# Attention with relative bias, then routed experts: keys and queries transposed two pairs ahead, and a smaller bias table fetched on another queue

## The chip, the cores and the metric

The kernel runs on one core of a Trainium2 chip. The metric is the time of one execution on the device, in microseconds (us); the median of three runs before the change is 409.79.

## What is computed

The reference has two parts. The first is attention with a bias that depends on the distance of query and key alone, through a table of 32 buckets per head:

```python
scores = scale * np.matmul(q, k.transpose(0, 1, 3, 2))      # 8 batches, 8 heads, 576 x 576, head size 64
bias = bias_table[bucket]                                   # bucket = f(|i - j|); constant from 128 on
scores = scores + bias.transpose(2, 0, 1)[None]
attn = softmax(scores)
out = np.matmul(attn, v)
```

The second takes the 4608 rows of that output (512 wide), sends each to one of 8 experts by a hash of its token id, and computes `relu(x @ w1[e]) @ w2[e]` for it.

## The kernel before

**Pairs.** Two heads of one batch make a pair; the 32 pairs (8 batches of 4) are gone through in order. The 576 positions are kept as four tiles of 128 (two row blocks T, each split by parity c of the position, so that a DMA row holds an even and an odd position) and a remainder of 64, which is collected for all heads of a batch. A pair has five groups: group g < 4 is one key tile against 512 queries, group 4 holds the remainder queries and remainder keys.

**One group on TensorE (PE).** `products` (line 457) multiplies the transposed keys `kz` with the transposed queries `qt` into the PSUM tile `ps`, of which there are three. `scores` (line 438, through the helper `bias`) adds the bias: a product of a reversed identity with a slice of `btb`, a band that holds the bias of every offset for every head; the remainder uses `btr`. ScalarE then takes the exponential of `ps` into `att` (line 492). The products of `att` with the values `va` run about seven groups later, nine at a time, into `px` (line 523); VectorE divides them into `x_all` (lines 532, 533).

**Transposes.** `cast_qk` turns the float32 loads `qf`, `kf` into `qh`, `kh` on GpSimd (POOL); `transpose_qk(n)` has PE transpose them into one PSUM tile `pqk` (line 373), which VectorE copies into `kz` (line 379, two copies) and `qt` (line 385). `pqk` shares its PSUM buffer with every second `px`. For the remainders of a batch, `load_rest` (lines 202, 214), `cast_rest` (line 246, giving `qrh`, `krh`) and `transpose_rest` (line 392, giving `pr`) do the same; `transpose_rest(b + 1)` stands in the third pair of batch b, behind group 1, and its casts stand in the second pair.

**Order.** Each engine runs its own list in the order of the program text (a manual schedule). In the main loop `pair_start(n)` issues on SyncE (SP) the loads of pair n + 4, in the first pair of a batch the next batch's remainders, and in pairs 2 to 11 one zero fill of the buffer `t_xperm`; on POOL the casts of pair n + 2, and later the scatter of finished rows. `behind(n, g)` follows each group: at g = 3 it transposes pair n + 1. POOL casts the values of pair n + 1 at g = 2. The buffers `qf`, `kf`, `vf` exist four times, `kz` three times, `qh`, `kh` and `qt` twice.

**Start.** Before the loop, PE multiplies the bias table `tbl` with a one-hot table `ohsb` (three parities of 384 columns, one product each, line 588). ScalarE copies the result in two pieces into `ebsb`, writes it to the DRAM buffer `t_f` (line 599), and reads it back: `btb` of heads 0 and 1 (`load_band`, line 605), `btr` in eight reads of 32 rows (line 618), later `btb` of heads 2 to 7, all on ScalarE's DMA queue. Each read takes a window that slides by one element per partition. The loads of q, k and v go on SP.

**After the loop** the rows are gathered by expert (`xpn`), transposed (`xps`), and multiplied with `w1t` (line 788) and `w2t` (line 806); finished rows are scattered to the output.

Of the kernel before, what the change touches and what calls it, by code (L numbers as in the profile page):

```python
# [11 lines left out]
F32 = mybir.dt.float32  # L12
# [19 lines left out]
def kernel(  # L32
# [38 lines left out]
    bucket = _bucket_table(NB, MAXD, S)  # L71
    last = NB - 1
    GL = 3 * P
    OH_np = np.zeros((NB, 3, GL), dtype=np.float32)
    for dl in range(3):
        for y in range(GL):
            r = 2 * (y - GL // 2 + 1) + dl - 1
            OH_np[bucket[min(abs(r), S - 1)], dl, y] += 1.0
            OH_np[last, dl, y] -= 1.0
    OH_np = OH_np.reshape(NB, 3 * GL)  # L80
    I128_np = np.zeros((P, 3, P), dtype=np.float16)
    I128_np[:, 0] = np.eye(P)
    I128_np[:, 1] = np.eye(P)[::-1]
# [65 lines left out]
    with tc.tile_pool(name="at", bufs=1) as at, tc.tile_pool(  # L149
# [18 lines left out]
        rr = [at.tile([P, (NPAIR + 1) * RC], F16, name=f"rr{i}")  # L168
              for i in range(2)]
        btb = at.tile([P, H, 3, WB], F16, name="btb")  # L170
        btr = at.tile([P, NPAIR, 2, D + RU], F16, name="btr")
        te = at.tile([P, NGT], I32, name="te")
        cnt = at.tile([P, 2 * P], F16, name="cnt")
        msk = at.tile([P, NGT + E], F32, name="msk")
# [192 lines left out]
        def transpose_qk(n, eng=None):  # L367
            pqk = aux(1, [P, 2, KT * P], F16, "pqk")
            for i, src in enumerate((kh, qh)):
                for t in range(KT):  # L370
                    T, c = t // 2, t % 2
                    o = P * t if i == 0 else NT * P * c + P * T
                    nc.tensor.transpose(  # L373
                        out=pqk[:, i, o : o + P],
                        in_=src[n][:, t, :, :].rearrange("p h d -> p (h d)"),
                        identity=ident[:, :],
                    )
            for hh in range(2):
                nc.vector.tensor_copy(  # L379
                    out=kz[n % 3][D * hh : D * hh + D, hh, :],  # L380
                    in_=pqk[D * hh : D * hh + D, 0, :],
                )
            kts[n] = kz[n % 3]
            qt = at.tile([P, KT * P], F16, name="qt", bufs=2)
            nc.vector.tensor_copy(out=qt[:, :], in_=pqk[:, 1, :])  # L385
            qts[n] = qt

# [30 lines left out]
        def rest_rest(b):  # L418
            prr = aux(0, [P, NPAIR, RC], F32, "prr")
            for m in range(NPAIR):  # L420
                nc.tensor.matmul(
                    out=prr[:, m, :], lhsT=kzr[b % 2][:, m, :],
                    rhs=qtr[b % 2][:, m, :], start=(m == 0), stop=True,
                    skip_group_check=True,
                )
            bias(
                prr[:, :, :].rearrange("p m (o u) -> p m o u", o=2),
                btr[:, :, :, D : D + RU], 2,
            )
            nc.scalar.activation(  # L430
                out=rr[b % 2][:, : NPAIR * RC].rearrange(
                    "p (m x) -> p m x", m=NPAIR
                ),
                in_=prr[:, :, :], func=AF.Exp, bias=0.0, scale=scale,
            )
# [27 lines left out]
        def scores(n, g):  # L463
            b, m = pairs[n]
            ps, att, qt = pss.pop((n, g)), atts[n], qts[n]
            T, c = g // 2, g % 2
            for hh in range(2):
                head = 2 * m + hh
                if g < KT:
                    x0 = D * T  # L470
                    bias(
                        ps[:, hh, :].rearrange("p (o u) -> p o u", o=2)[
                            :, :, x0 : x0 + BW
                        ],
                        btb[:, head, 1 - c : 3 - c,
                            D * (1 - T) : D * (1 - T) + BW], 1,
                    )
                    continue
                nc.tensor.matmul(
                    out=ps[:, hh, 2 * P :], lhsT=kzr[b % 2][:, m, :],  # L480
                    rhs=qt[:, 2 * P * hh : 2 * P * hh + 2 * P],
                    start=False, stop=True, skip_group_check=True,
                )
                for t in range(KT - 2, KT):
                    bias(
                        ps[:, hh, RC * t : RC * t + RC].rearrange(
                            "p (o u) -> p o u", o=2
                        ),
                        btb[:, head, 1 - t % 2 : 3 - t % 2, BW : BW + RU], 1,
                    )  # L490
                bias(ps[:, hh, 512 - D :], btr[:, m, hh, :D], 2)
            nc.scalar.activation(  # L492
                out=att[:, g, :, :], in_=ps[:, :, :],
                func=AF.Exp, bias=0.0, scale=scale,
            )
# [74 lines left out]
        load(0, "k")  # L570
        tbl = at.tile([NB, H], F32, name="tbl")
        nc.scalar.dma_start(out=tbl[:, :], in_=bias_table)
        ohsb = at.tile([NB, 3 * GL], F32, name="ohsb")
        nc.scalar.dma_start(out=ohsb[:, :], in_=OH_d.ap())
        nc.scalar.dma_start(out=idents[:, :, :], in_=I128_d.ap())
        load(0, "q")
# [2 lines left out]
        def z_init(i):  # L579
            nc.gpsimd.memset(kz[i][D:P, 0, :], 0.0)  # L580
            nc.gpsimd.memset(kz[i][:D, 1, :], 0.0)

        z_init(0)
        cast_qk(0, nc.vector, nc.vector)
        bps = [slot("bps") for _ in range(2)]
        ebsb = at.tile([H, 3, GL], F16, name="ebsb")
        for i in range(3):
            nc.tensor.matmul(
                out=bps[i // 2][:H, i % 2, :GL], lhsT=tbl[:, :],
                rhs=ohsb[:, GL * i : GL * i + GL],  # L590
            )
        for i in range(2):
            w = 2 - i
            nc.scalar.activation(
                out=ebsb[:, 2 * i : 2 * i + w, :],
                in_=bps[i][:H, :w, :GL], func=AF.Copy, bias=0.0,
                scale=1.0 / scale,
            )
# [5 lines left out]
        def load_band(h0, h1):  # L604
            nc.scalar.dma_start(
                out=btb[:, h0:h1, :, :].rearrange("p h a w -> p (h a) w"),
                in_=bass.AP(
                    F_d.ap().tensor, h0 * 3 * GL,
                    [[1, P], [GL, 3 * (h1 - h0)], [1, WB]],
                ),  # L610
            )

        load_band(0, 2)
        for hh in range(2):
            for c in range(2):
                for o in range(2):
                    r0 = D * hh + RU * c
                    nc.scalar.dma_start(
                        out=btr[r0 : r0 + RU, :, o, :],
                        in_=bass.AP(  # L620
                            F_d.ap().tensor,
                            (3 * hh + o - c + 1) * GL + P - RU,
                            [[1, RU], [6 * GL, NPAIR], [1, D + RU]],
                        ),
                    )
        transpose_qk(0)
        load(0, "v")
        load(1, "qk")
        for i in range(2):
            nc.gpsimd.memset(kzr[i][:, :, :].bitcast(I32), 0)  # L630
            nc.gpsimd.memset(vt[i][:, :, :].bitcast(I32), 0)
# [8 lines left out]
        for i in range(3):  # L640
            nc.gpsimd.memset(va[i][:, :, D : D + 1], 1.0)
        cast_v(0)
        load_rest(0, "v")
        load(1, "v")
        cast_qk(1)
        z_init(1)
        cast_vrest(0)
        load_band(2, H)
        load(2)
        load(3)  # L650
        z_init(2)
        nc.sync.dma_start(out=msk[:, :], in_=MSK_d.ap())
# [31 lines left out]
        def pair_start(n):  # L684
            b, m = pairs[n]
            if n + 4 < NP:
                load(n + 4)
            if n == 4:
                route_load()
            if 2 <= n < 2 + FILLS:  # L690
                fill_table(n - 2)
            if b + 1 < B and m == 0:
                load_rest(b + 1)
            if n + 2 < NP:
                cast_qk(n + 2)
# [12 lines left out]
            if n == 22:  # L708
                load_w2(0)
            if n == 25:  # L710
                load_w1(1)
            if n == 28:
                load_w2(1)

        def behind(n, g):
# [12 lines left out]
                advance(av, 9)  # L728
            if g == 2 and n + 1 < NP:
                cast_v(n + 1)  # L730
            if g == 3 and n + 1 < NP:
                transpose_qk(n + 1)

        for n in range(NP):
            pair_start(n)
            for g in range(NIT):
                products(n, g)
                scores(n, g)
                behind(n, g)
        advance(av, 99)  # L740
        assert not waiting
        guard.__exit__(None, None, None)
# [215 lines left out]
```

## Time and profile before

| | |
|---|---|
| median of three runs | 409.79 us (408.8 to 410.69) |
| profiled execution | 408.63 us, of which the span of the trace is 406.7 |
| mean granted TensorE clock | 0.972 of full speed |
| busy: PE / ScalarE / POOL / VectorE | 86% / 52% / 41% / 33% of the span |
| DMA | 72.66 MB, 179 GB/s in the mean |
| start, up to ScalarE's first exponential | 0 to 24.0 us |
| attention pairs | to about 231 us |
| gap until the first expert product | to about 250 us |
| experts | to 406.7 us |

Busy times are sums over stages that have different limits; what a wait is worth is read from the stage in which it stands. Line numbers are those of the kernel before.

### The profile page before, as it was taken

How to read it: one execution, taken by the hardware profiler on the slowest of the kernel's cores; microseconds unless marked ns; L12 is line 12 of the kernel's file. 1: busy time of each engine (PE TensorE's matmuls, PEld its weight loads, DVE VectorE, ACT ScalarE, POOL GpSimd, SP SyncE). 2: the span in 40 equal slices, each digit the busy share in tenths (PEclk: the TensorE clock that was granted, in tenths of full speed). 3: DMA queues.
4: the chain of work that ended last, by engine and by line, in shares of the span. 5: the costliest groups of instructions: out<-in, count | busy, mean ns of one | idle time of the engine just before them, and what ended most of it. 6: DMA issues, size and time to landing. Idle time of an engine off the chain costs nothing.

```text
span 406.7 us, 9256 instructions
## 1 busy us (share of the span) xinstructions
PE 351.2 (86%) x3792; PEld 229.0 (56%) x3792; DVE 136.2 (33%) x339; ACT 211.4 (52%) x235; POOL 167.1 (41%) x248
## 2 busy tenths in 40 slices
PE   4278999899999999999999807999999999999990
PEld 1035666566666666666666605665657575656650
DVE  1211346544434444344443401323140413223220
ACT  2046877687787877878778601322415051423320
POOL 3713225242576666583846040152333515151331
PEclk9998999999999999999999966999999999999997
DMA  6795967969685755997984025399999999995211
GB/s 172 192 244 147 266 134 215 272 189 269 196 237 169 206 176 134 249 186 212 235 174 94 10 77 175 53 204 159 258 161 266 201 193 261 160 264 115 89 70 61
DMA packets 95107, 72.66 MB, mean 179 GB/s; under 512 B 16295, under 2 KB 86183, under 8 KB 95056
## 3 DMA queue, kind: packets, MB, share of 16 engines
q0 software_dynamic: 17664, 30.96, 36.1%
q1 hardware_dynamic: 72880, 38.98, 35.1%
q10 hardware_dynamic: 4512, 2.04, 2.0%
q8 instruction: 32, 0.52, 0.5%
q14 instruction: 19, 0.16, 0.1%
HBM read 69.27 MB, written 21.03 MB: 222 GB/s over the span
## 4 chain that ended last, share of the span: by engine, by line
PE 71%; DVE 10%; DMA 8%; ACT 4%; issue 2%; SPq 2%; POOL 1%; POOLq 0%; ACTq 0%; DVEq 0%
PE hps L788 17%; PE ops L806 17%; PE ps L457 13%; PE ps L438 9%; PE px L523 8%; DVE kz L379 6%; ACT att L492 3%; PE pqk L373 3%; DVE qt L385 3%; PE xps L767 2%; DMA btb<-t_f 2%; DMA qf<-in_q_dram 2%; DMA xpn<-t_xperm 1%; DMA btr<-t_f 1%; SPq L188 1%
## 5 line engine op out<-in xcount | busy, mean ns | idle before, releaser
L492 ACT ACTIVATE att<-ps 128x1024 f16<-128x1024 f32 x160 | 161.7, 1023 | 58.6 <-PE ps L438 41.8
L794 ACT ACTIVATE h<-hps 128x640 f16<-128x640 f32 x64 | 45.0, 704 | 112.9 <-PE hps L788 112.9
L457 PE MATMUL ps<-qt,kz 128*128 128x512 f16 x256 | 78.9, 391 | 15.4 <-DVE qt L385 13.9
L438 PE MATMUL ps<-btb,idents 128*128 128x384 f16 (+1 forms) x384 | 78.2, 288 | 8.8 <-DMA btb<-t_f 8.8
L806 PE MATMUL ops<-w2t,h 128*128 128x512 f16 x320 | 72.7, 379 | 0.0
L788 PE MATMUL hps<-xpt,w1t 128*128 128x320 f16 x512 | 72.1, 301 | 0.1
L523 PEld LDWEIGHTS <-att 128*128 128x128 f16 x1408 | 61.0, 98 | 18.6 <-ACT rr L430 3.5
L523 PE MATMUL px<-va,att 128*128 128x65 f16 x1280 | 64.6, 193 | 1.2 <-DVE rcp L532 0.4
L438 PEld LDWEIGHTS <-idents 128*128 128x128 f16 x456 | 39.7, 100 | 42.0 <-issue 12.4
L814 POOL DMA_INDIRECT out_dram<-ok,xpn x40 | 39.2, 980 | 57.4 <-DVE ok L813 51.3
L788 PEld LDWEIGHTS <-w1t 128*128 128x128 f16 x512 | 50.4, 99 | 21.2 <-issue 0.3
L379 DVE COPY kz<-pqk 64x512 f16<-64x512 f16 x64 | 27.0, 422 | 77.6 <-PE pqk L373 76.6
L806 PEld LDWEIGHTS <-h 128*128 128x128 f16 x320 | 30.8, 98 | 33.4
L548 POOL DMA_INDIRECT t_xperm<-x_all,ds x40 | 39.4, 985 | 21.9 <-DVE rcp L532 11.3
L813 DVE COPY ok<-ops 128x512 f32<-128x512 f32 x40 | 27.7, 692 | 47.0 <-PE ops L806 47.0
L457 PEld LDWEIGHTS <-kz 128*128 128x128 f16 x512 | 28.2, 99 | 22.2 <-DVE qt L385 18.7
L771 DVE COPY xpt<-xps 128x640 f16<-128x640 f16 x32 | 15.0, 488 | 74.2 <-PE xps L767 59.7
L226 POOL CAST qh<-qf 128x512 f16<-128x512 f32 x31 | 19.0, 613 | 42.9 <-PE pqk L373 25.5
L533 DVE TENSOR_TENSOR x_all<-px,rcp 128x384 f16<-128x384 f32 x64 | 31.4, 491 | 2.2
L234 POOL CAST va<-vf 128x512 f16<-128x512 f32 x32 | 20.0, 624 | 28.5 <-PE px L523 15.7
L132 POOL DMA_DIRECT2D w1t<-in_moe_w_dram x8 | 6.5, 810 | 52.0 <-PE xps L767 51.9
L532 DVE RECIPROCAL rcp<-px 128x6 f32<-128x6 f32 x64 | 11.7, 183 | 42.4 <-PE px L523 42.4
(72 smaller groups left out, 243.0 us busy)
## 6 DMA issues: line engine op xcount, KB each, us to landing
kf<-in_k_dram SPq DMA_DIRECT2D x64, 128.0 KB
qf<-in_q_dram SPq DMA_DIRECT2D x64, 128.0 KB
vf<-in_v_dram SPq DMA_DIRECT2D x64, 128.0 KB
w1t<-in_moe_w_dram POOLq DMA_DIRECT2D x8, 1024.0 KB, 9.6
w2t<-in_moe_w_dram POOLq DMA_DIRECT2D x8, 1024.0 KB, 10.4
t_xperm<-zx SPq DMA_DIRECT2D x10, 514.0 KB
xpn<-t_xperm SPq DMA_DIRECT2D x8, 642.5 KB
btb<-t_f ACTq DMA_DIRECT2D x1, 1152.0 KB
```

The costliest lines, as they stand in the source:

```text
L379: nc.vector.tensor_copy(out=kz[n % 3][D * hh : D * hh + D, hh, :], in_=pqk[D * hh : D * hh + D, 0, :],)
L438: nc.tensor.matmul(out=out, lhsT=idents[:, which, :], rhs=rhs, start=False, stop=True, skip_group_check=True,)
L457: nc.tensor.matmul(out=ps[:, hh, o : o + rhs.shape[1]], lhsT=lhsT, rhs=rhs, start=(g < KT or t == 0), stop=True, skip_group_check=True,)
L492: nc.scalar.activation(out=att[:, g, :, :], in_=ps[:, :, :], func=AF.Exp, bias=0.0, scale=scale,)
L523: nc.tensor.matmul(out=po, lhsT=lhsT, rhs=rhs, start=(i == 0), stop=(i == len(todo) - 1), skip_group_check=True,)
L533: nc.vector.tensor_tensor(out=x_all[:, b, its[0] : its[0] + ni, :DM].rearrange("p t (m h d) -> p t m h d", h=2, m=NPAIR)[:, :, m, :, :], i ...
L548: sc_in = nc.gpsimd.indirect_dma_start(out=xperm_d.ap()[:, :], out_offset=bass.IndirectOffsetOnAxis(ap=ds2[:, B * t + b : B * t + b + 1], ...
L788: nc.tensor.matmul(out=hps[:, nr, :NR], lhsT=w1h[:, kt, ts(ft, P)], rhs=xt[e][:, kt, ts(nr, NR)], start=(kt == 0), stop=(kt == NPT - 1),)
L794: nc.scalar.activation(out=h1[:, ft, :].rearrange("p (r n) -> p r n", r=NRC), in_=hps[:, :, :NR], func=AF.Relu, bias=0.0, scale=1.0,)
L806: nc.tensor.matmul(out=ops[:, :], lhsT=h1[:, ft, ts(kc, P)], rhs=w2h[:, ft, :], start=(ft == 0), stop=(ft == NFT - 1),)
L813: nc.vector.tensor_copy(out=ok[:, :], in_=ops[:, :])
L814: so = nc.gpsimd.indirect_dma_start(out=out[:, :], out_offset=bass.IndirectOffsetOnAxis(ap=xn[e][:, kc, DM:XW].bitcast(I32), axis=0), in_= ...
```

## The change

The loads, casts and transposes keep their places in the loop but work for a later pair: the casts of pair n + 3 and the transposes of pair n + 2 stand where those of n + 2 and n + 1 stood, with a third `qt`. Pair 1 is transposed after the first group of pair 0, and pair 2 is cast before the loop. The one-hot table holds only the 129 columns per parity in which the bias differs from its far value; the rest of `ebsb` is zeroed by a memset on POOL. One product and one copy take the place of three and two. `btr` becomes a tile with a row of 480 elements per head pair, read by four transfers on SP; both parities are slices (`bro`) of that row. The band of heads 0 and 1 stays on ScalarE's queue, heads 2 and 3 and heads 4 to 7 are read on SP. In SP's order the loads of v of pair 0 and q, k of pair 1 stand before the `btr` reads, the remainders and pair 1's v after the second band.

```diff
-    OH_np = np.zeros((NB, 3, GL), dtype=np.float32)          # GL = 384
+    GN = MAXD + 1                                            # 129
+    OH_np = np.zeros((NB, 3, GN), dtype=np.float32)
...
-        btr = at.tile([P, NPAIR, 2, D + RU], F16, name="btr")
+        btr = at.tile([P, NPAIR, GL + D + RU], F16, name="btr")
+        bro = [btr[:, :, GL * o : GL * o + D + RU] for o in range(2)]
...
-            qt = at.tile([P, KT * P], F16, name="qt", bufs=2)
+            qt = at.tile([P, KT * P], F16, name="qt", bufs=3)
...                                                            # rest_rest
-            bias(prr[:, :, :].rearrange("p m (o u) -> p m o u", o=2), btr[:, :, :, D : D + RU], 2)
+            for o in range(2):
+                bias(prr[:, :, RU * o : RU * o + RU], bro[o][:, :, D : D + RU], 2)
...
+        ebsb = at.tile([H, 3, GL], F16, name="ebsb")
+        nc.gpsimd.memset(ebsb[:, :, :], 0.0)
...
-        for i in range(3):
-            nc.tensor.matmul(out=bps[i // 2][:H, i % 2, :GL], lhsT=tbl[:, :],
-                             rhs=ohsb[:, GL * i : GL * i + GL])
-        for i in range(2):
-            w = 2 - i
-            nc.scalar.activation(out=ebsb[:, 2 * i : 2 * i + w, :], in_=bps[i][:H, :w, :GL], ...)
+        bps = slot("bps")
+        nc.tensor.matmul(out=bps[:H, 0, : 3 * GN], lhsT=tbl[:, :], rhs=ohsb[:, :])
+        nc.scalar.activation(out=ebsb[:, :, P - 1 : P - 1 + GN],
+                             in_=bps[:H, 0, : 3 * GN].rearrange("h (a b) -> h a b", a=3), ...)
...
-        load_band(0, 2)
+        load_band(0, 2, nc.scalar)
+        load(0, "v")
+        load(1, "qk")
         for hh in range(2):
             for c in range(2):
-                for o in range(2):
-                    r0 = D * hh + RU * c
-                    nc.scalar.dma_start(out=btr[r0 : r0 + RU, :, o, :], in_=bass.AP(
-                        F_d.ap().tensor, (3 * hh + o - c + 1) * GL + P - RU,
-                        [[1, RU], [6 * GL, NPAIR], [1, D + RU]]))
+                r0 = D * hh + RU * c
+                nc.sync.dma_start(out=btr[r0 : r0 + RU, :, :], in_=bass.AP(
+                    F_d.ap().tensor, (3 * hh + 1 - c) * GL + P - RU,
+                    [[1, RU], [6 * GL, NPAIR], [1, GL + D + RU]]))
         transpose_qk(0)
-        load(0, "v")
-        load(1, "qk")
...
         cast_v(0)
+        cast_qk(1)
+        z_init(1)
+        load_band(2, 4, nc.sync)
         load_rest(0, "v")
         load(1, "v")
-        cast_qk(1)
-        z_init(1)
         cast_vrest(0)
-        load_band(2, H)
         load(2)
+        load_band(4, H, nc.sync)
+        cast_qk(2)
         load(3)
...                                                            # pair_start, behind, main loop
-            if n + 2 < NP:
-                cast_qk(n + 2)
+            if n + 3 < NP:
+                cast_qk(n + 3)
...
-            if g == 3 and n + 1 < NP:
-                transpose_qk(n + 1)
+            if g == 3 and n + 2 < NP:
+                transpose_qk(n + 2)
...
                 behind(n, g)
+                if (n, g) == (0, 0):
+                    transpose_qk(1)
```

## Rows read from the trace of the kernel before

**Rows 1.** The chain that ended last, shares of the span by engine.
```profile
PE 71%; DVE 10%; DMA 8%; ACT 4%; issue 2%; SPq 2%; POOL 1%; POOLq 0%; ACTq 0%; DVEq 0%
```

**Rows 2.** Waits for `qt`: whole run, PE from 66.3, PE from 93 (us, times, longest).
```profile
PE ps L457 <- DVE qt L385: 13.9, 31, 1.0
...
PE ps L457 <- DVE qt L385: 11.4, 25, 1.0
...
PE ps L457 <- DVE qt L385: 9.0, 21, 0.4
```

**Rows 3.** Busy times in stretches of four pairs (PE, PEld, DVE, ACT, POOL, clock, DMA, GB/s).
```profile
40.64:66.28 25.64, 23.84 (x351) 16.69 (x349) 11.96 (x34) 20.51 (x22) 7.44 (x14) 1.00 0.76 192
...
93.00:118.58 25.58, 23.77 (x351) 16.69 (x350) 10.92 (x31) 20.52 (x22) 12.62 (x20) 1.00 0.86 225
```

**Rows 4.** Timeline between two pairs (start, us, engine, line, idle before).
```profile
103.91 0.42 DVE L385 COPY qt<-pqk 128x512 f16<-128x512 f16 x1
...
104.39 0.61 PE L457 MATMUL ps<-qt,kz 128*128 128x512 f16 x2 [0.43 <-DVE qt L385]
...
105.16 0.43 PE L523 MATMUL px<-va,att 128*128 128x65 f16 x9
```

**Rows 5.** Timeline of ScalarE and its DMA queue (ACTq) at the start.
```profile
8.49 0.48 ACT L594 ACTIVATE ebsb<-bps 8x384 f16<-8x384 f32 x1 [0.48 <-PE bps L588]
10.92 0.50 ACTq L599 DMA_DIRECT2D t_f<-ebsb  x1
13.24 0.45 ACTq L605 DMA_DIRECT2D btb<-t_f  x1
13.73 9.29 ACTq L618 DMA_DIRECT2D btr<-t_f  x8
...
24.02 3.79 ACT L492 ACTIVATE att<-ps 128x1024 f16<-128x1024 f32 x4 [15.05 <-DMA btr<-t_f]
```

**Rows 6.** Timeline of PE at the start.
```profile
4.46 3.99 PE L588 MATMUL bps<-ohsb,tbl 32*8 32x384 f32 x6 [4.46 <-DMA ohsb<-t_bias_oh]
...
19.74 0.80 PE L438 MATMUL ps<-btb,idents 128*128 128x384 f16 x2 [6.68 <-DMA btb<-t_f]
...
25.09 1.01 PE L457 MATMUL ps<-qt,kz 128*128 128x512 f16 x2 [1.57 <-ACT att L492]
...
31.80 0.48 PE L438 MATMUL ps<-btb,idents 128*128 128x384 f16 x2 [2.11 <-DMA btb<-t_f]
```

**Rows 7.** Timeline of SyncE's DMA queue (SPq) at the start.
```profile
7.34 0.98 SPq L188 DMA_DIRECT2D kf<-in_k_dram  x2
...
15.83 3.21 SPq L188 DMA_DIRECT2D qf<-in_q_dram  x2
...
27.06 5.24 SPq L202 DMA_DIRECT2D qr<-in_q_dram  x2
```

**Rows 8.** SyncE's own waits: whole run, then 60 to 100, then 100 to 235.
```profile
SPq L202 <- DMA btb<-t_f: 4.1, 1, 4.1
...
SPq L188 <- POOL va L234: 0.6, 1, 0.6
...
SPq L188 <- POOL va L234: 13.9, 6, 3.1
```

**Rows 9.** Timeline of GpSimd: the casts of the remainder keys.
```profile
37.27 0.40 POOL L246 CAST krh<-kr 128x256 f16<-128x256 f32 x1 [1.79 <-DMA kr<-in_k_dram]
...
64.59 0.40 POOL L246 CAST krh<-kr 128x256 f16<-128x256 f32 x1 [1.55 <-DMA kr<-in_k_dram]
...
88.75 0.40 POOL L246 CAST krh<-kr 128x256 f16<-128x256 f32 x1 [1.38 <-DMA kr<-in_k_dram]
```

**Rows 10.** Timeline of PE: the transposes of the remainder keys.
```profile
40.64 0.27 PE L392 MATMUL pr<-idents,krh 128*128 128x128 f16 x2
...
66.28 0.28 PE L392 MATMUL pr<-idents,krh 128*128 128x128 f16 x2
...
93.00 0.27 PE L392 MATMUL pr<-idents,krh 128*128 128x128 f16 x2
```

More of the change, by code (lines that the diff above doesn't have):

```diff
@@ L73 @@
     GL = 3 * P
-    OH_np = np.zeros((NB, 3, GL), dtype=np.float32)
+    GN = MAXD + 1
+    OH_np = np.zeros((NB, 3, GN), dtype=np.float32)
     for dl in range(3):
-        for y in range(GL):
-            r = 2 * (y - GL // 2 + 1) + dl - 1
+        for y in range(GN):
+            r = 2 * y - MAXD + dl - 1
             OH_np[bucket[min(abs(r), S - 1)], dl, y] += 1.0
             OH_np[last, dl, y] -= 1.0
-    OH_np = OH_np.reshape(NB, 3 * GL)
+    OH_np = OH_np.reshape(NB, 3 * GN)
     I128_np = np.zeros((P, 3, P), dtype=np.float16)
@@ L170 @@
         btb = at.tile([P, H, 3, WB], F16, name="btb")
-        btr = at.tile([P, NPAIR, 2, D + RU], F16, name="btr")
+        btr = at.tile([P, NPAIR, GL + D + RU], F16, name="btr")
+        bro = [
+            btr[:, :, GL * o : GL * o + D + RU] for o in range(2)
+        ]
         te = at.tile([P, NGT], I32, name="te")
@@ L425, in rest_rest @@
                 )
[L426 to L429, printed above, removed]
+            for o in range(2):
+                bias(
+                    prr[:, :, RU * o : RU * o + RU],
+                    bro[o][:, :, D : D + RU], 2,
+                )
             nc.scalar.activation(
@@ L490, in scores @@
                     )
-                bias(ps[:, hh, 512 - D :], btr[:, m, hh, :D], 2)
+                bias(ps[:, hh, 512 - D :], bro[hh][:, m, :D], 2)
             nc.scalar.activation(
@@ L572 @@
         nc.scalar.dma_start(out=tbl[:, :], in_=bias_table)
-        ohsb = at.tile([NB, 3 * GL], F32, name="ohsb")
+        ohsb = at.tile([NB, 3 * GN], F32, name="ohsb")
+        ebsb = at.tile([H, 3, GL], F16, name="ebsb")
+        nc.gpsimd.memset(ebsb[:, :, :], 0.0)
         nc.scalar.dma_start(out=ohsb[:, :], in_=OH_d.ap())
@@ L584 @@
         cast_qk(0, nc.vector, nc.vector)
-        bps = [slot("bps") for _ in range(2)]
-        ebsb = at.tile([H, 3, GL], F16, name="ebsb")
-        for i in range(3):
[L588 to L591, printed above, removed]
-        for i in range(2):
-            w = 2 - i
[L594 to L598, printed above, removed]
+        bps = slot("bps")
+        nc.tensor.matmul(
+            out=bps[:H, 0, : 3 * GN], lhsT=tbl[:, :], rhs=ohsb[:, :],
+        )
+        nc.scalar.activation(
+            out=ebsb[:, :, P - 1 : P - 1 + GN],
+            in_=bps[:H, 0, : 3 * GN].rearrange("h (a b) -> h a b", a=3),
+            func=AF.Copy, bias=0.0, scale=1.0 / scale,
+        )
         nc.scalar.dma_start(
@@ L602, with load_band @@
         )
-        def load_band(h0, h1):
-            nc.scalar.dma_start(
+        def load_band(h0, h1, eng):
+            eng.dma_start(
                 out=btb[:, h0:h1, :, :].rearrange("p h a w -> p (h a) w"),
@@ L611, in load_band @@
             )
-        load_band(0, 2)
+        load_band(0, 2, nc.scalar)
+        load(0, "v")
+        load(1, "qk")
         for hh in range(2):
             for c in range(2):
-                for o in range(2):
-                    r0 = D * hh + RU * c
[L618 to L625, printed above, removed]
+                r0 = D * hh + RU * c
+                nc.sync.dma_start(
+                    out=btr[r0 : r0 + RU, :, :],
+                    in_=bass.AP(
+                        F_d.ap().tensor, (3 * hh + 1 - c) * GL + P - RU,
+                        [[1, RU], [6 * GL, NPAIR], [1, GL + D + RU]],
+                    ),
+                )
         transpose_qk(0)
-        load(0, "v")
-        load(1, "qk")
         for i in range(2):
```

## The prediction

> **What bounds the kernel now.** I read the chain of work that ended last first. TensorE (PE) carries 71% of the span, but 10% lies on VectorE, which a kernel bound by products alone would not show [rows 1]. The waits say where that comes from: the first product of a pair, line 457, waits for the copy `qt` 31 times, 13.9 us in total [rows 2]. Then the stretches by batch: from one batch's `pr` transposes to the next, four pairs take 25.6 us, of which PE is busy 23.8, and ScalarE 20.5 [rows 3]. The 1.8 us between are four waits of 0.45. One of them in the timeline: `qt` is copied 103.91 to 104.33, and the next pair's first product starts at 104.39 after 0.43 us of idling [rows 4]. So the middle of the kernel is PE work plus one exposed copy for each pair.
>
> The start is another matter, read from ScalarE's queue. It ends the second half of `ebsb` at 8.97, but issues the write of `t_f` at 10.92, spends 13.73 to 23.02 on issuing eight `btr` reads, then the large `btb` read, and does its first exponential at 24.02, after 15.05 us of idling that the view puts down to `btr` [rows 5]. PE waited 6.68 us to 19.74 for the first band, 1.57 to 25.09 for ScalarE and 2.11 to 31.80 for the second band [rows 6]. SyncE's queue (SP) has holes of its own: the two `qf` issues at 15.83 take 3.21 us, and the two `qr` issues at 27.06 take 5.24 us [rows 7], where two undisturbed ones take about 1.0; 4.1 us of the latter is a wait for `btb`, a transfer that `qr` has no data from [rows 8]. An issue can thus stand for an older, unrelated transfer.
>
> Last, what would be late if PE came earlier. PE needs the casts of the remainders, `krh`, at its `pr` transposes. For batches 1, 2 and 3 GpSimd starts that cast at 37.27, 64.59 and 88.75, after idling for the transfer [rows 9], and PE starts `pr` at 40.64, 66.28 and 93.00 [rows 10]. With the cast's 0.40 the spare time is 2.97, 1.29 and 3.85 us.
>
> **The change, part by part.** *Transposes and casts two pairs ahead.* No instruction is added: eight transposes and three copies per pair stay at the same place behind group 3, only for the pair after. The copy `qt` then has a whole pair to finish in, covered by about 5.9 us of PE work (23.8 / 4), so the 31 waits go to nothing. If they came back, each would cost 0.45. What is late next on PE is the first `px` that needs the same PSUM buffer: it stands at 105.16 with the wait, so at 104.73 without it, and the copy ends at 104.33 [rows 4]; 0.4 us is left. ScalarE's 20.5 us per batch fits into 23.8. On GpSimd the casts keep their place in each pair; what they need is loaded one pair less ahead. 25 of the waits, 11.4 us, come after the `pr` of batch 2 at 66.28; of these 9.0 come after that of batch 3 at 93.00 [rows 2].
>
> *One-hot product and the write of `t_f`.* Six partial products over 3 x 384 columns take 3.99 us [rows 6]; 387 columns are two of them, 1.33. Two copies become one, of 387 columns like the 0.48 us one of 384 [rows 5]. `ebsb` is thus ready near 4.46 + 1.33 + 0.48 = 6.3 instead of 8.97. The write may be held by an older transfer, as it was for 1.95 us: issue at 6.3 to 8.5. In the old run it let `btb` go at 13.24, 2.3 us after its issue [rows 5]; so the band's read goes out at about 8.6 to 10.8, some 3.5 us earlier. The added memset on GpSimd lies in its idle start.
>
> *`btr` in four reads on SP, the large band in two, both on SP.* ScalarE loses 9.3 us of issuing, so its first exponential follows the first band. PE's own lead, if nothing else were late, is by 66.28: 3.5 (band) + 1.6 (the wait for ScalarE) + 2.1 (second band) + 2.5 (the 31 - 25 copies before 66.28, 13.9 - 11.4) = 9.7 us [rows 2, 6].
>
> *What SP pays.* Four `btr` and two band reads come onto its queue: six issues at about 0.5, 3.0 us. The first stands before the write of `t_f` has landed; behind it wait the remainders of v, pair 1's v, pairs 2 and 3. The write lands 2.3 us after its issue, at 8.6 to 10.8; SP's last issue ahead of `btr` ends at 8.3 [rows 7], so it idles 0.3 to 2.5 us, say 1.1. The four reads move 480 columns per row for the 192 before, 491 KB for 197; the smaller one-hot table saves 98. Net 0.2 MB, about 0.9 to 1.0 us at the 192 to 225 GB/s of the batch stretches [rows 3], partly under SP's idle time: I take 0.3. What SP can win back is 4.1 us (the wait for `btb`, now split and earlier) and 2.2 us (the `qf` hole). Everything won would be 6.3; what I count as paid is 3.0 + 1.1 + 0.3 = 4.4. No row shows how the waits for older transfers fall in the new order; I take all 6.3 as won, because the long reads now stand further from `qr`, and so a lead of 6.3 - 4.4 = about 2 us. The bounds are -6 (nothing won; 3.0 + 2.5 + 0.9 paid) and +6 (all won, the new issues falling into SP's idle times).
>
> *Where PE meets SP.* From 60 to 100 us SP waited for GpSimd only 0.6 us [rows 8]: its loads come at their own pace and do not come faster because PE is ahead. Hence the remainders of batch 2 move by SP's lead only, and PE can be ahead at its `pr` by at most 1.29 + 2 = 3.3 us, though it would be 9.7 free. The other 6.4 us become new waits of PE: for `krh` of batch 1 first (2.97 + 2 = 5.0 at most), then batch 2. At batch 3 the limit is 3.85 + 2 = 5.85, and 3.3 + (11.4 - 9.0) = 5.7 passes just below. Past 100 us SP waits six times, 13.9 us, for the casts of v [rows 8], thus for compute, and the limit is gone. The eight batches' extra `prr` bias product (two of 128 columns for one of 256) costs at most 0.4 in all.
>
> Sum: 3.3 + 11.4 - 0.4 = 14.3 us. The profiled execution took 408.63 (span 406.7 and 1.9 around it), so 394.3; the median of the runs shown is 409.79, 1.16 above it, so 395.5.
>
> One rule speaks against the start's part of this. The Trainium skill, "DMA: Bandwidth & Descriptors", section "Issuing engines are not separate DMA queues", says that transfers started by different engines run on the same 16 DMA engines and interleave, so that another issuer saves only issue time, usually small beside the transfer. By that rule SP would have no lead, and the sum would be the second rival's below. The trace agrees only in part: the issue time was 9.29 us here [rows 5], not small.
>
> **The rivals.** *Transfers, not queues, set the pace.* The same bytes come when they came before, the lead is 0. Then PE gains 1.3 by batch 2, 3.7 by batch 3, and 9.0 - 0.4 after: 12.3 us, 397.5. For it: SP's free run and the DMA engines' 0.76 to 0.86 busy share in those stretches [rows 3]. Against it: SP's two holes, in which it issued nothing.
>
> *Supply hardly binds.* With SP's lead at its upper bound, 6, batch 2 allows 7.3, batch 3 then 7.3 + 2.4 = 9.7 (under 3.85 + 6): 9.7 + 9.0 - 0.4 = 18.3 us, 391.5. With 8.4 or more PE keeps all its 9.7: 9.7 + 11.4 - 0.4 = 20.7 us, 389. For it: the sum of the waits. Against it: spare times of 1.3 and 3.9 us.
>
> *SP comes out later.* With a lead of -6, batch 2 is at 1.29 - 6 = -4.7, batch 3 at -4.7 + 2.4 = -2.3, and 9.0 - 0.4 follow: 6.3 us, 403.5; with -3, 9.3 us, 400.5. For it: six more issues and the wait for `t_f` ahead of pairs 2 and 3.
>
> *The copy still holds PE,* by the shared PSUM buffer after it, when VectorE's routing steps or its divisions come in between. The 13.9 us stay, the start gives up to 1.3 + 2: near 407.5 to 409. Against it: 0.4 us of room.
>
> *Slower: SP behind `t_f`.* SP is one queue in order; if the reads of `btr` hold it until the old landing near 13.2 and every later issue waits for older transfers again, each microsecond of lateness past the spare time goes to PE one for one. By batch 2's row it decides from 1.29 + 11.4 - 0.4 = 12.3 us of lateness; at 14.5 the loss passes 0.5%, a time of 412. The rows bear out 6.
>
> **How the numbers follow.** My forecast 0.42 (393 to 397), no lead 0.20, supply hardly binds 0.14, SP later 0.14, the copy stays 0.05, slower 0.05. The likeliest gives 395.5. The first three and the nearer half of SP later hold 0.83, which gives 388.5 to 402 with the bounds of the lead. Faster by over 0.5% (2 us, about what a measurement of this kernel tells from no change): 0.42 + 0.20 + 0.14 + 0.14 + 0.01 = 0.91; within it 0.04; slower 0.05.
>
> **What would show it.** Right: no wait of line 457 for `qt`; four pairs in about 23.8 us late in the attention; first exponential near 17 instead of 24.02; new PE waits for `krh` at line 392 in pairs 2 and 6, together 5 to 7 us; the expert stage as long as before. Wrong: the `qt` wait replaced by one at line 523; no wait at line 392 (then the time is near 389 to 391); PE waits for `kh` or `btb` in pairs 0 to 3; SP's `qr` of batch 1 issued after 31.77.

## The result, and the profile after

The changed kernel took 395.24 us in the median of four runs (392.37 to 398.82), against 409.58 us for the kernel before beside it (408.80 to 410.69). Medians here are of all runs and ratios of the fast runs alone, without those over 1.5% above their kernel's fastest (398.82 here, three more in e10 and e11). The ratio is 0.9625, with a 95% interval of 0.9554 to 0.9695. Two later sets of six runs gave 398.49 us (ratio 0.9725, 0.9690 to 0.9759) and 395.90 us (0.9676, 0.9651 to 0.9701). The gain is therefore 10.5 to 14.3 us, and the changed kernel varies more from run to run than the one before. The profiled execution is the slowest of the first four: 398.82 us, a span of 396.7, which is 10.0 less than before. The two later profiles took 399.00 and 399.89, so all that is read from traces below explains a gain of about 10 us; what the executions of 392 to 396 us do differently, no trace shows. Line numbers moved on by 4 or 5 (188 is now 192, 392 is 396, 457 is 462, 523 is 528).

The chain of work that ended last, shares of the span by engine, answers to [rows 1]:

```profile
PE 52%; DMA 21%; SPq 13%; POOL 5%; issue 4%; DVE 2%; ACT 1%; POOLq 0%; DVEq 0%; ACTq 0%
```

VectorE, 10% before, is down to 2%. In its place the chain runs through transfers and SyncE's queue: 34% together, where it was 10%. Beside PE's own work, what set the end before was the exposed copy of each pair; now, for a third of the span, it is transfers and the queue that issues them, the supply of data.

TensorE's waits in the whole run (us, times, longest), against [rows 2]:

```profile
PE pr L396 <- POOL krh L250: 9.6, 3, 5.8
PE ps L443 <- DMA btb<-t_f: 4.0, 1, 4.0
...
PE px L528 <- DVE qt L389: 2.6, 1, 2.6
PE pqk L377 <- POOL kh L230: 2.5, 2, 1.4
```

The 31 waits of the first product for `qt` are gone without exception. New among the long ones are those for casts of loaded data, `krh` and `kh` on POOL, and one wait of `px`.

Stretches from one batch's `pr` to the next (columns as in [rows 3]):

```profile
91.41:114.57 23.16, 23.08 (x352) 16.71 (x351) 10.92 (x31) 20.43 (x22) 10.78 (x18) 1.00 0.81 230
114.57:137.72 23.15, 23.07 (x351) 16.71 (x350) 10.91 (x31) 20.53 (x22) 17.24 (x26) 1.00 0.69 199
137.72:160.88 23.16, 23.08 (x352) 16.72 (x350) 10.92 (x31) 20.54 (x22) 16.86 (x25) 1.00 0.88 219
```

Four pairs went from 25.6 to 23.16 us, so 0.60 to 0.62 for each pair, although the idle time that disappeared was only 0.45. Even PE's busy time fell, from 23.8 to 23.08, with no product left out. The timeline of PE between two pairs shows how:

```profile
101.24 0.35 PE L528 MATMUL px<-va,att 128*128 128x65 f16 x6
101.43 0.33 PE L528 MATMUL px<-vt,att 128*128 128x130 f16 x3
101.60 0.59 PE L462 MATMUL ps<-qt,kz 128*128 128x512 f16 x2
```

The same place in the kernel before; the row that follows it is the product at 104.39 in [rows 4]:

```profile
103.44 0.35 PE L523 MATMUL px<-va,att 128*128 128x65 f16 x6
103.63 0.33 PE L523 MATMUL px<-vt,att 128*128 128x130 f16 x3
```

From the start of the three `px` products to the start of the next product it was 104.39 - 103.63 = 0.76; now it is 101.60 - 101.43 = 0.17. The `px` group counts as busy for 0.33, but its successor starts after 0.17 when nothing holds it. The wait cost its idle 0.43 and also the 0.16 of overlap that was lost ahead of it.

The start: ScalarE with its DMA queue (against [rows 5]) in the timeline:

```profile
5.24 1.28 ACT L596 ACT_TABLE_LOAD   x1 [5.24 <-PE bps L593]
6.54 0.48 ACT L596 ACTIVATE ebsb<-bps 8x387 f16<-8x387 f32 x1
7.72 0.50 ACTq L601 DMA_DIRECT2D t_f<-ebsb  x1
10.87 0.43 ACTq L607 DMA_DIRECT2D btb<-t_f  x1
15.94 1.02 ACT L497 ACTIVATE att<-ps 128x1024 f16<-128x1024 f32 x1 [8.92 <-PE ps L443]
```

The first exponential comes at 15.94 where it came at 24.02. SyncE's queue (against [rows 7]):

```profile
10.87 1.76 SPq L621 DMA_DIRECT2D btr<-t_f  x4
...
16.90 1.54 SPq L192 DMA_DIRECT2D qf<-in_q_dram  x2
...
21.05 1.86 SPq L192 DMA_DIRECT2D qf<-in_q_dram  x2
22.95 1.91 SPq L192 DMA_DIRECT2D kf<-in_k_dram  x2
...
28.79 1.82 SPq L192 DMA_DIRECT2D kf<-in_k_dram  x2
...
31.73 1.15 SPq L206 DMA_DIRECT2D qr<-in_q_dram  x2
32.98 1.11 SPq L206 DMA_DIRECT2D kr<-in_k_dram  x2
```

The two long holes are gone, but four issues of two now take 1.5 to 1.9 us instead of 1.0, and `qr` of batch 1 still goes out only at 31.73 (before, its two issues stood in the queue from 27.06 to 32.30). So the casts of the remainder keys come when they came before (timeline of GpSimd, against [rows 9]):

```profile
37.78 0.40 POOL L250 CAST krh<-kr 128x256 f16<-128x256 f32 x1 [1.84 <-DMA kr<-in_k_dram]
64.76 0.40 POOL L250 CAST krh<-kr 128x256 f16<-128x256 f32 x1 [1.14 <-DMA kr<-in_k_dram]
88.22 0.40 POOL L250 CAST krh<-kr 128x256 f16<-128x256 f32 x1 [1.09 <-DMA kr<-in_k_dram]
```

And PE, which without the 5.75 us of waiting would reach batch 1's `pr` at 32.49, 8.15 us ahead of the kernel before, gives most of that back (timeline of PE, against [rows 10]):

```profile
38.24 0.40 PE L396 MATMUL pr<-idents,krh 128*128 128x128 f16 x2 [5.75 <-POOL krh L250]
65.22 0.28 PE L396 MATMUL pr<-idents,krh 128*128 128x128 f16 x2 [1.03 <-POOL krh L250]
91.41 0.28 PE L396 MATMUL pr<-idents,krh 128*128 128x128 f16 x2
...
187.01 0.29 PE L396 MATMUL pr<-idents,krh 128*128 128x128 f16 x2 [2.81 <-POOL krh L250]
```

PE is ahead of the kernel before by 2.40, 1.06 and 1.59 us at the `pr` of batches 1, 2 and 3, by 4.01, 6.43, 8.84 and 8.28 at those of batches 4 to 7, and by 10.8 at the first transpose of the expert stage (235.90 against 246.69).

### The profile page after: what moved, and what is told of

It is laid out like the page before. It is cut to its first block, busy times and chain, and to the rows that moved or that the text cites. A ratio compares the mean times of both kernels' runs of the same rounds, so it can differ in the third digit from the quotient of the medians.

```text
span 396.7 us, 9264 instructions
## 1 busy us (share of the span) xinstructions
PE 346.4 (87%) x3796; PEld 229.8 (58%) x3796; DVE 135.4 (34%) x339; ACT 210.6 (53%) x234; POOL 169.1 (43%) x249
## 4 chain that ended last, share of the span: by engine, by line
PE 52%; DMA 21%; SPq 13%; POOL 5%; issue 4%; DVE 2%; ACT 1%; POOLq 0%; DVEq 0%; ACTq 0%
PE hps L792 18%; PE ops L810 17%; SPq L192 6%; PE ps L462 5%; DMA vf<-in_v_dram 4%; PE px L528 4%; PE ps L443 3%; DMA kr<-in_k_dram 3%; DMA t_xperm<-zx 3%; SPq L206 3%; DMA kf<-in_k_dram 3%; PE xps L771 3%; DMA vr<-in_v_dram 2%; POOL t_xperm L553 2%; SPq L218 2%
## 5 line engine op out<-in xcount | busy, mean ns | idle before, releaser
L528 PE MATMUL px<-va,att 128*128 128x65 f16 x1280 | 65.5, 195 | 4.2 <-DVE qt L389 2.6
L792 PEld LDWEIGHTS <-w1t 128*128 128x128 f16 x512 | 50.8, 99 | 21.4
L462 PEld LDWEIGHTS <-kz 128*128 128x128 f16 x512 | 29.3, 99 | 0.8 <-issue 0.7
L771 PE MATMUL xps<-idents,xpn 128*128 128x128 f16 x160 | 13.9, 230 | 13.1 <-DMA xpn<-t_xperm 12.9
L238 POOL CAST va<-vf 128x512 f16<-128x512 f32 x32 | 19.9, 623 | 10.7 <-PE px L528 5.2
```

Of the source, the lines that this page charges most:

```text
L462: nc.tensor.matmul(out=ps[:, hh, o : o + rhs.shape[1]], lhsT=lhsT, rhs=rhs, start=(g < KT or t == 0), stop=True, skip_group_check=True,)
L528: nc.tensor.matmul(out=po, lhsT=lhsT, rhs=rhs, start=(i == 0), stop=(i == len(todo) - 1), skip_group_check=True,)
L792: nc.tensor.matmul(out=hps[:, nr, :NR], lhsT=w1h[:, kt, ts(ft, P)], rhs=xt[e][:, kt, ts(nr, NR)], start=(kt == 0), stop=(kt == NPT - 1),)
```

## The experiments

All were timed in five rounds beside the kernel before on their chip. The first four and the last four ran where the kernel before took 408.99 and 408.69 us; the middle four on a chip where it took 414.58, so they are compared by ratio; the changed kernel itself was not run on that chip. My theory: **supply**. PE's advance up to about 90 us is set by when SyncE's loads land; the start part of the change has nothing to give, and the gain is mainly the copies'. Its rivals: the start part brings part of the gain; or what is left is a matter of order, and other transfers ahead of the needed ones can be moved away.

**The changed kernel again (e0),** unedited.

> The changed kernel once more, for a second profile and a tighter ratio. Supply theory (SyncE's stream of loads sets when TensorE may pass the remainder transposes, about 38.2 and 65.2 us into the span whatever TensorE does): the wait for krh in pair 2 is again 5 to 6 us and the transposes of batch 2 start again within 1 us of 65.2; what differs between executions is the wait at batch 7 (2.8 us in the first profile) and the routing wait of 2.6 us at 73 us. Rival (clock theory: the half clock after the long wait is what moves the time between executions): the transposes of batch 2 start at a time that varies by 2 us or more. Time 392 to 397 either way.

398.49 us, ratio 0.9725 (0.9690 to 0.9759). PE's longest waits stand where they stood: 6.03 us before batch 1's `pr`, 2.66 at `px` in pair 6. The reference for the next three.

**The loop part alone (e1).** The kernel before with

```diff
-            if n + 2 < NP:
-                cast_qk(n + 2)
+            if n + 3 < NP:
+                cast_qk(n + 3)
...
-            if g == 3 and n + 1 < NP:
-                transpose_qk(n + 1)
+            if g == 3 and n + 2 < NP:
+                transpose_qk(n + 2)
...
+                if (n, g) == (0, 0):
+                    transpose_qk(1)
```

(with a third `qt`, and `cast_qk(2)` before the loop).

> The kernel before with the loop part alone: casts three pairs and transposes two pairs ahead, a third qt, pair 1 transposed behind the first group, pair 2 cast before the loop; one-hot table, btr and bands as before. Supply theory: the remainder keys land when they did before (37.1 and 64.5), TensorE passes batch 2's transposes at 65.1 to 65.5, and every later pair saves 0.45 to 0.6 us: 393 to 398, the same as the whole change within 3 us; the start part is worth nothing by itself. Rival (the start is worth the 7 to 8 us by which ScalarE's first exponential came earlier): 400 to 405, slower than the whole change by 5 us or more.

398.68 us, ratio 0.9721 (0.9686 to 0.9756): the whole change's 398.49 within 0.2. PE's waits:

```profile
PE ps L438 <- DMA btb<-t_f: 11.2, 2, 6.3
PE pr L392 <- POOL krh L246: 4.5, 2, 2.5
```

PE waits 11.2 us for the bands, 7.5 more than in e0, and yet the kernel ends as early: its waits for `krh`, for `kh` and of `px` for `qt` are 5.3 us together, where e0 has 14.2. What PE loses to the bands it doesn't lose to what comes late behind them.

**The start part alone (e2).** The changed kernel with the casts and transposes one pair later again (the edit above reversed).

> The whole change at the start (one-hot over 129 columns, one product and copy, btr in four reads and the later bands on SyncE, later loads), but casts two pairs and transposes one pair ahead in the loop as before, with pair 2's cast at pair_start(0) again. Supply theory: first exponential near 16 us, but batch 2's remainder transposes still at 65.2 to 66, and the 25 waits for qt after that are back: 0 to 1.5 us under the kernel before, 408 to 410. Rival (the start is worth 7 to 8 us): 401 to 403.

407.83 us, ratio 0.9969 (0.9956 to 0.9981): 1.2 us. PE's waits:

```profile
PE ps L462 <- DVE qt L389: 14.4, 31, 1.0
PE pr L396 <- POOL krh L250: 8.0, 1, 8.0
```

The first band's product is at 15.03 (it was at 19.74), and one wait of 8.0 us before 38.04 swallows it. e1 and e2 together decide for supply: the start is worth 1.2 us alone, and beside the loop part nothing that the runs can tell (0.2 us, where each ratio is uncertain by 1.4 us).

**The remainders a batch earlier (e3).** The changed kernel with

```diff
         load(3)
+        load_rest(1)
...
-            if b + 1 < B and m == 0:
-                load_rest(b + 1)
+            if b + 2 < B and m == 3:
+                load_rest(b + 2)
```

(and `cast_rest` ahead of `cast_qk`).

> The changed kernel with the remainders of a batch loaded earlier: batch 1's right after pair 3's loads, those of batch b + 2 in the last pair of batch b (so batch 2's ahead of the token loads of pair 4), and GpSimd casts the remainders ahead of the next keys and queries. No work is added. Supply theory: the waits for krh at batches 1, 2 and 7 (5.75 + 1.03 + 2.81 in the first profile) shrink to 0 at batches 2 and 7; at batch 1 part of it comes back as a wait of 1 to 4 us for kh, since the same bytes are in front; with a shorter idle the half clock after it goes too. 385 to 391. Rival (the remainders are not what binds; the loads of pairs 9 and later are as late): waits of the same length appear for kh in pairs 3 to 8, time within 2 us of the changed kernel.

396.05 us, ratio 0.9667 (0.9642 to 0.9692), 2.4 us under e0 where much more was expected. The waits for `krh` are down to 0.2 us (its casts at 31.51, 54.82 and 82.27), but others took their place. PE's waits:

```profile
PE pqk L377 <- POOL kh L230: 7.8, 4, 2.9
PE px L528 <- DVE qtr L413: 4.3, 1, 4.3
```

VectorE's wait behind the second of them:

```profile
DVE te L287 <- DMA te<-in_moe_token_ids_dram: 5.1, 1, 5.1
```

What was moved up pushed back what now stands behind it: the heads' own keys, and the token ids for the routing, on which VectorE stands with the copy `qtr` queued behind it.

**The routing later (e4).** The changed kernel with the steps of the routing in pairs 8 to 11 instead of 6 to 11, with the memsets of `keep` before the loop.

```diff
-            if 6 <= n < 12:
+            if 8 <= n < 12:
```

> The changed kernel with the routing steps on VectorE spread over pairs 8 to 11 instead of 6 to 11, and the two memsets of keep on GpSimd moved to the start. The order of the loads is as in the change. If the wait of 2.6 us of the products px for qt near 73 us comes from VectorE standing in its routing scan until GpSimd, which is late by its own waits for loads, has set keep: that wait goes, the waits for krh stay (6, 1 and 1 to 3 us), 395.5 to 396.5. Rival (the wait is of the copies themselves, which come too close to the next px): it stays, 398 to 399.

Ratio 0.9695 (0.9657 to 0.9732). The 2.6 us wait of `px` in pair 6 is gone, and so is the wait before batch 2's `pr` (1.38 before batch 7's and 5.20 before batch 1's are left). Yet the time is not measurably below the changed kernel's three ratios. On this chip four pairs took 26.80 us from 111.24 on, with PE busy 23.77, where 23.16 had been seen. PE's waits in that stretch are those of `px` for `qtr`, `qt` and `rr`, 2.9 us together; why VectorE and ScalarE came late there stays open.

**Remainders early and routing later (e5),** both edits.

> The earlier remainders and the later routing together. In the run with earlier remainders alone, TensorE passed batch 2 at 59.2 instead of 65, and then stood 4.3 and 1.9 us behind VectorE, which waited in its routing for the token ids and for keep. Supply theory: both go, what is late next is kh of pairs 8 to 10 by 1 to 2 us; 389 to 392. Rival (the loads of the whole stretch are simply late and each removed wait comes back for the next transfer): 394 to 396.5.

Ratio 0.9666 (0.9632 to 0.9700), no better than e3 alone. PE waits for `kh` six times, 7.9 us in all, the longest 2.0.

**The reads of `btr` behind the loads of pair 2 (e6),** meant to keep SyncE from standing behind the write of `t_f`.

```diff
         load(2)
+        for hh in range(2):
+            for c in range(2):
+                ...                     # the four btr reads, moved here
         load_band(4, H, nc.sync)
```

> The changed kernel with the four btr reads moved on SyncE behind the loads of pair 2, so that the remainders of v, pair 1's v and pair 2 no longer stand behind the write of t_f (the second band still does). If the idle time of SyncE behind t_f (2.1 us in the first profile) is what ate its lead: batch 1's and batch 2's krh come 1.5 to 2.5 us earlier, 396 to 397. If the loads' own pace sets them: batch 2's krh within 1 us of 64.5, 397.5 to 399; a wait for btr in group 4 of pair 0 may appear.

Ratio 0.9706 (0.9671 to 0.9742). `krh` is cast at 39.03 and 65.41, no earlier than in the changed kernel (37.78, 64.76), and PE waits 2.24 us for `btr` besides. But this does not test SyncE's idling: the read of the second band also needs the write and still stands ahead of the loads, so SyncE idled 2.0 us as before, from 8.72 to 10.75. A second hole came from 14.12 to 16.51, a wait of 2.4 us for `btb`, and `qr` of batch 1 went out at 33.12, later than the 31.73 of the changed kernel. What the idling costs stays open.

**The experts' weights spread out (e7).** e5 with the four weight loads (1 MB each) in pairs 14, 18, 22 and 28 rather than 20, 22, 25 and 28.

> The kernel with earlier remainders and later routing, and the four weight loads of the first two experts issued in pairs 14, 18, 22 and 28 instead of 20, 22, 25 and 28. If the wait of 1 to 3 us for kh or krh near 187 to 196 us comes from those 1 MB loads beside the loads of q, k and v: it shrinks under 1 us and the time is 1 to 3 us under the version without it. Rival (it comes from the pace of SyncE's queue alone): no difference beyond 1 us.

Ratio 0.9672 (0.9639 to 0.9706), as e5. The longest wait near 190 us is 1.07 us, where e5 has 1.24. That the weights play a part in the late waits is not shown.

**The same bytes in more transfers (e8).** The changed kernel with each load of v in four transfers of 64 KB instead of two of 128:

```diff
+                    if key == "v":
+                        for T in range(NT):
+                            nc.sync.dma_start(out=dst[n][:, hh, T, :], ...)
+                        continue
```

> The changed kernel, with each pair's v load issued as four transfers of 64 KB instead of two of 128 KB: the same bytes, two more issues of some 0.5 us on SyncE for each pair. If the pace of SyncE's loads is set by the number of its issues: krh of batch 2, cast at 64.5 to 64.8 us in the two profiles of the changed kernel, comes at 70 to 73 us, with a wait of TensorE of 6 to 8 us before batch 2's pr, and the time is 4 to 8 us above the changed kernel's on the same chip. If it is set by the bytes that all queues move: krh within 1 us of where it was, and the time within 2 us.

417.32 us, ratio 1.0199 (1.0176 to 1.0223): slower than the kernel before, and 21.4 us over the changed kernel on the same chip, for 64 more transfers of the same rows, 0.33 us each. GpSimd's timeline:

```profile
41.91 0.40 POOL L262 CAST krh<-kr 128x256 f16<-128x256 f32 x1 [1.99 <-DMA kr<-in_k_dram]
71.53 0.40 POOL L262 CAST krh<-kr 128x256 f16<-128x256 f32 x1 [2.30 <-DMA kr<-in_k_dram]
97.17 0.40 POOL L262 CAST krh<-kr 128x256 f16<-128x256 f32 x1 [1.14 <-DMA kr<-in_k_dram]
```

In the changed kernel on the same chip (e11) these casts start at 36.25, 62.33 and 87.54; here they come 5.7, 9.2 and 9.6 us later, and 19.7 later at batch 7. PE's wait for them in the whole run:

```profile
PE pr L408 <- POOL krh L262: 23.2, 5, 7.9
```

It is 10.5 in e11. Two stretches of 30 to 215 us, first e11's, then e8's (columns as in [rows 3]):

```profile
30.00:215.00 185.00, 169.94 (x2482) 121.39 (x2480) 81.05 (x235) 146.06 (x150) 97.36 (x153) 0.96 0.78 201
```

```profile
30.00:215.00 185.00, 160.09 (x2260) 113.41 (x2260) 75.14 (x218) 131.89 (x136) 88.51 (x142) 0.93 0.73 190
```

The DMA engines are less busy (0.73 for 0.78) and move fewer bytes per second (190 GB/s for 201) while PE waits more. So the bytes are not what limits e8; the number of transfers in SyncE's queue is. That queue is nearly full even in e11: from 38 to 65 us its 41 issues, taken one by one, add up to 23.6 of 27 us, with a median of 0.47; without what single issues took beyond 0.6 it would be 20.3. So most of it is plain issuing, and a smaller part issues that were held. The two profiled executions are 18.7 us apart in span: 12.7 are longer waits for `krh`, and the lower granted clock, which falls in and behind these waits, is worth an estimated 5.6 (0.03 x 185). The direction was the issue theory's, the size three times what I had expected of it: I had counted the delay once, up to batch 2, but it goes on growing.

**The zero fills later (e9).** Two fills in each of pairs 7 to 11 instead of one in each of pairs 2 to 11.

```diff
-            if 2 <= n < 2 + FILLS:
-                fill_table(n - 2)
+            if 7 <= n < 12:
+                fill_table(2 * n - 14)
+                fill_table(2 * n - 13)
```

> The changed kernel, with the ten zero fills (0.5 MB each) issued two in each of pairs 7 to 11 instead of one in each of pairs 2 to 11. If bytes set the pace of SyncE's loads: some 1.5 to 2 MB less stand before the remainders of batches 1 and 2, at some 217 GB/s 7 to 9 us; krh of batch 2 is cast 4 us or more earlier, and the waits for krh before batch 1 and 2 shrink from 6.0 and 1.0 to under 3 and to nothing; a part of it comes back as a wait in pairs 8 to 12, so the time is 1 to 4 us under the changed kernel's. If issues set it: krh 1 to 1.5 us earlier and the time within 1.5 us of the changed kernel's.

401.31 us, ratio 0.9819 (0.9787 to 0.9850): 5.4 us slower than the changed kernel beside it. With three fills, 1.5 MB, less ahead of it `krh` of batch 2 is cast at 61.79: 0.5 us earlier than in e11 (62.33) and 3.0 earlier than in the first profile (64.76), where the changed kernel's own profiles differ by 2.4. Bytes would have given 4 us or more; neither theory had the time longer. A wait of 4.51 us before batch 6's `pr` is new. It doesn't explain the time: the profiled executions of e9 and e11 are only 1.0 us apart (400.91 and 399.89). Why the fills' new place costs 5.4 us in the median I haven't settled.

One row of SyncE's queue in the changed kernel's first profile also says that few bytes can cost much:

```profile
52.35 5.81 SPq L275 DMA_DIRECT2D te<-in_moe_token_ids_dram  x6
```

These are the token ids for the routing, six transfers of 18 KB in all, and they stand right ahead of the remainders of batch 2 and their fill. They take the queue for 5.81 us (5.24 in e11), of which the third issue alone takes 3.02 (2.10); what held it the trace doesn't show. e3 passed them with the remainders; moving the token ids themselves was not tried.

**Everything at once (e10).** Remainders early, routing later, fills later: the candidate to beat both.

> The changed kernel, with the remainders of the next batch issued a batch earlier, the routing steps in pairs 8 to 11 with their memsets at the start, and the zero fills two in each of pairs 7 to 11: the candidate that is to beat both. If the waits left in the first 90 us are a matter of which bytes go first: they shrink by 4 to 8 us against the changed kernel, ratio 0.950 to 0.962 to the kernel before. If total bytes before about 90 us set the end of that stretch whatever their order: ratio 0.965 to 0.970, as with the remainders early and the routing later.

396.55 us, ratio 0.9686 (0.9655 to 0.9718). Up to 100 us PE's largest wait after the bands is 2.13 us, but then 3.18 comes before batch 4's `pr` and 3.53 before batch 7's. The time is the changed kernel's: none of the orders tried removed the waits, they came back later in the attention.

**The changed kernel a third time (e11),** beside e8 to e10.

> The changed kernel once more, on the same chip as the three others, for comparison: ratio to the kernel before 0.9625 to 0.9725, as in its two runs so far; TensorE's longest waits before batch 1's pr (5.5 to 6.1 us) and at px in pair 6 (2.5 to 2.7 us).

395.90 us, ratio 0.9676 (0.9651 to 0.9701). Waits of 5.93 before batch 1's `pr`, 2.42 at `px` in pair 6 and 3.60 before batch 7's.

## Why the prediction was right, and where not

The time was right, 395.24 for 395.5, and so was the mechanism of the main term. But terms of the sum were off in opposite directions, the later sets gave 398.5 and 395.9, and no profile shows a run as fast as the forecast: the agreement to 0.3 us is partly luck.

**The 31 waits go to nothing: right. Their size: too small.** I took the idle column's 0.45 for each; the stretches show 0.60. The 25 waits behind batch 2's `pr` are worth 25 x 0.60 = 15 us, not 11.4. The starts of two rows of the kernel before, 0.76 us apart for a group that needs 0.17, would have told it. The Trainium skill, "TensorE: Matmul & The Clock Gate", section "Step-by-step: what each phase is for", says that the drain of a product overlaps the fill of the next, so that a product that stands alone costs more than one in a stream; the trace agrees, with 0.16 us here.

**The start: right, by somewhat different numbers.** `ebsb` was ready at 7.02, not 6.3, because ScalarE's table load of 1.28 us, in its idle time before, now stands behind the wait for `bps`. The write went out at 7.72 (forecast 6.3 to 8.5), released the band's read 3.15 us later rather than 2.3, and the first exponential came at 15.94 (near 17).

**SP's lead of 2: this step failed.** It was -0.5, -0.2 and +0.5 us at the casts of batches 1 to 3. I had taken "all 6.3 as won". The two holes did close, but 3.2 us came back as slower issues at 16.90, 21.05, 22.95 and 28.79, and SyncE idled 2.1 us behind the write of `t_f`, not 1.1. How much of the lead each of the two cost is not shown, since e6 left the idling where it was.

Why an issue stands for an unrelated transfer, for which the prediction had no row, the traces do hold. The program's transfers on SyncE and ScalarE take eight semaphores in turn, both queues together, and an issue waits until the previous transfer on its semaphore has landed. The kernel before's `qr` at 31.77 had the semaphore of the `btb` read that ScalarE issued at 23.59, and e6's `qf` at 16.51 that of the first band's read at 10.76.

One of the prediction's signs of being wrong, `qr` of batch 1 issued after 31.77, was missed by 0.04 us here and met in e0 (32.25). The first rival, a lead of 0 (the paragraph on the Trainium skill calls it the second), described this term better, but what the runs show speaks against its reason: 1.5 MB less brought `krh` forward by 3.0 us at most (e9), and more transfers of the same bytes put it back by 9.2 (e8). The rule that I weighed, that issue time is usually small beside the transfer, does not fit here either: SyncE's issues fill 23.6 of 27 us in e11. The Trainium skill's "DMA: Bandwidth & Descriptors", section "Rules for kernel authors", which wants many small transfers made into a large one, is borne out by e8, whose added transfers cost 0.33 us each.

**Where PE meets SP: right.** With the measured lead the rule gives 1.29 - 0.2 = 1.1 at batch 2; PE was 1.06 ahead. The waits for `krh` in pairs 2 and 6 were 5.75 + 1.03 = 6.8 (forecast 5 to 7). e1 and e2 confirm that nearly all that the start gains goes there.

**The room of 0.4 before `px`: right, but for one pair.** In pair 6 VectorE stood in the routing, waiting for a memset on GpSimd that stood behind casts that waited for loads. The timeline:

```profile
70.50 0.82 DVE L314 TENSOR_TENSOR_SCAN inc<-keep,rps 128x320 f32<-128x320 f32 x1 [3.00 <-POOL keep L297]
...
72.62 0.43 DVE L389 COPY qt<-pqk 128x512 f16<-128x512 f16 x1
...
73.11 0.45 PE L528 MATMUL px<-va,att 128*128 128x65 f16 x9 [2.57 <-DVE qt L389]
```

It cost 2.57 us, which I had as a rival (the copy still holds PE) for every pair. e4 removes it without a gain in time that the runs show.

**"Past 100 us the limit is gone": not quite.** Batch 7's `pr` waited 2.81 us (1.16 and 3.60 in the two other profiles). It looks as if a PE that no longer stalls meets the pace of the loads again; no run isolates the cause.

The sum, redone from this profile: 1.06 + 15 - 2.57 - 2.81 = 10.7, against 10.8 us at the start of the expert stage. Left out are three terms that cancel: the low clock behind the last wait (0.54 granted from 187.0 to 190.5, an estimated loss of 1.6), the gap ahead of the experts, shorter by 0.6 (12.87 for 13.48), and 1.1 that the kernel before lost in batch 2's four pairs (26.72 us, where others took 25.6). The expert stage itself took 160.8 for 160.0. The forecast had 14.3 = 3.3 + 11.4 - 0.4. No version that was tried stands clear of the changed kernel's three ratios (0.9625 to 0.9725). Fewer and larger loads, which e8 points to, were not tried.

## What to carry over

A stall's cost is read from the distance between starts with and without it, not from the idle time in front of the waiting instruction alone. Before counting an engine's advance as gain, look for the next thing that it needs and for what sets that thing's time; here a start 8 us shorter was worth 1.2 us alone and nothing measurable beside the loop part, since the loads came no sooner. Where one queue in order fed everything, moving transfers within it only moved the wait, and one test with the same bytes in more transfers told whether bytes or transfers were the limit. An experiment that moves one of two instructions with the same wait, as e6 did, leaves the wait where it was; its trace tells.

## What was not expected of the hardware

- Cutting 64 loads of 128 KB into 128 of 64 KB, with the same rows of 512 bytes, cost 21.4 us, while the DMA engines' busy share from 30 to 215 us fell from 0.78 to 0.73.
- A wait of PE costs more than itself through the clock. Late in the 5.75 us wait before batch 1's `pr`, at 37.10, the granted clock fell to half (1.2 GHz of 2.4) and stayed there until 43.90; the pair of 512-column products took 1.06 us instead of 0.59. PE's 5.66 us of work in that window would have taken an estimated 2.8 at the full clock. The window of the changed kernel's profile:

```profile
37.10:43.90 6.80, 5.66 (x46) 3.87 (x47) 1.38 (x5) 1.95 (x2) 3.56 (x7) 0.50 0.87 250
```

- The kernel before took 408.7 to 409.6 us on three occasions and 414.6 on a fourth, on another chip, so times from different occasions can differ by 1.4% with no change in the kernel.
